# Pooled attention and a gated dense layer on one core: scores of two pairs in one step, an earlier due date for g, other places for the last tiles, and a new table of shifts

## The chip, the cores and the metric

The kernel runs on 1 core of one Trainium2 chip. The metric is the device time of that core in microseconds (us). Names of engines: PE is TensorE, ACT is ScalarE, DVE is VectorE, POOL is GpSimd, SP is SyncE, which here only issues DMAs.

## What is computed

```python
# attention: batch 8, heads 8, seq 576, head_dim 64
k_p = k.reshape(B, H, Sp, pool, D).mean(axis=3)          # pool = 8, Sp = 72
v_p = v.reshape(B, H, Sp, pool, D).mean(axis=3)
scores = scale * np.matmul(q, k_p.transpose(0, 1, 3, 2))  # scale = 1 / 8
scores = scores - np.max(scores, axis=-1, keepdims=True)
attn = np.exp(scores)
attn = attn / (np.sum(attn, axis=-1, keepdims=True) + 1e-09)
attn_out = np.matmul(attn, v_p)
# dense part: 4608 tokens, w_in 512 x 2048, w_out 2048 x 512
x = attn_out.transpose(0, 2, 1, 3).reshape(B * S, H * D)
h = x @ w_in
g = h * (1.0 / (1.0 + np.exp(-1.702 * h)))
out = g @ w_out
```

The result has 4608 rows of 512. Each batch has 576 tokens.

## The kernel before

**The work.** For each of 8 batches the attention is computed first. `sum_keys` and `sum_values` pool keys and values over 8 (tiles red_k, red_v, spread into kbd and vbd, and turned by PE into kps); the last 8 of the 72 pooled rows go a way of their own: they are loaded into tl, summed into tred, spread into tbd. `scores` runs the queries in two pieces: piece 0 has two tiles of 128 tokens, piece 1 has two of 128 and one of 64. For each of four head pairs j one step on PE computes the scores of a piece (sps, L665), DVE takes the maxima (nm) and subtracts them (sc), ACT takes the exponential, DVE the sums (sm) and the products main and tail. `weigh` turns the weights (mt, or apt and tpt on PE in batches 0 and 1; batches from TURNED = 2 on are turned on DVE), splits them into a high and a low part (ah and al, at), multiplies them by the values (pav, L876 to L879) and splits the result into x, high and low. The 8 x 64 tokens left over from the batches form chunk 8, which `gather_left` collects at the end.

`dense` runs over chunks c = 0 to 8 of 512 tokens and steps f = 0 to 15 of 128 columns of w_in. For one f, 12 matmuls give h (three products of high and low parts for each of four blocks of the depth, L1066 to L1068). ACT computes g (L1081) and its rounded form gh (L1086) from h; POOL, or DVE in chunk 8, computes gl = g - gh (L1094). Then, in a block of 12 matmuls, gh and gl times w_out are added to four output tiles o_0, o_128, o_256 and o_384 (L1111 to L1113), which stay in PSUM through all 16 steps. The fourth tile of chunk 0 is called warm. After f = 15 each tile is copied to SBUF (osb, L1123) and stored (L1124, queue of ACT). In chunk 8 tiles 0 and 256 are copied by DVE and stored by SP in two DMAs each, tiles 128 and 384 by ACT and its queue (L1127, L1130).

**Places.** PSUM has four tiles for o (ps_o), two for h and two for the attention (ps_a). In SBUF the place "g" has one buffer, which g and the copies osb_0 and osb_256 share; "osb" has two buffers, for osb_128 and osb_384; "gh" has two.

**What sets the order.** All steps go to a planner, `Plan.order`, which simulates the engines and lays out each engine's instructions in one fixed order by due dates. `plan.due` is set ahead of each part of the code; the table `SHIFTS` adds microseconds to the due dates of steps of one kind ("DVE tred2_0" is the step on DVE that writes tred for batch 2, part 0). A round of one batch's attention beside one chunk has 96 us. Before 58 us the planner fills PE's gaps with small matmuls of the identity (`keep_warm`, L1214). On the chip each engine runs its instructions in that order and waits at semaphores for what it needs.

Of the kernel before, what the change touches and what calls it, by code (L numbers as in the profile page):

```python
# [23 lines left out]
COLD = 7.0  # L24
UNTIL = 58.0
# [7 lines left out]
    "ACT at1_1": 15, "ACT g0_256": 16, "ACT gh0_0": 10, "ACT vh0": -26, "DMA kv2_0": 11, "DMA tl1": 13,  # L33
    "DVE at0_1": 14, "DVE e": 20, "DVE kbd1": 42, "DVE nm0_1": 6, "DVE nm1_0": 24, "DVE raws": 4, "DVE tail0_0": 13,
    "DVE tail0_1": 3, "DVE tbd1": 26, "DVE vbd2": -18, "DVE vt1": 4, "PE h0_256": -4, "PE h1_0": -3.4,
    "PE kps1_0": -70, "PE kps1_1": 53, "PE o1_384": -11, "PE qps0_1": 5, "PE red1_1": 13, "PE sps2_0": -7,
    "PE tpt0_1": -19, "PE tpt1_0": 21,
# [215 lines left out]
def attention_moe_kernel(ctx: ExitStack, tc: tile.TileContext, q, k, v, w_in, w_out, out):  # L253
# [371 lines left out]
    def scores(b, piece, m, whole_q=None):  # L625
# [8 lines left out]
        sm = buf(att, [P, NT, H], F32, "sm", f"sm{n}")  # L634
        for j in range(NJ):
# [25 lines left out]
            ps = buf(ps_o if first else ps_a, [P, 512], F32, "o" if first else "a", f"sps{n}_{j}")  # L661

            def score(j=j, qt=qt, ps=ps):
                for t, (s0, ns) in enumerate(tiles):
                    nc.tensor.matmul(  # L665
                        ps()[:ns, t * PW : (t + 1) * PW],
                        lhsT=qt()[:, s0 - o0 : s0 - o0 + ns],
                        rhs=m.k2()[:, j],
                        start=True,
                        stop=True,  # L670
                    )

            pe(246 * len(tiles), score, [qt, (m.k2, j // NP)], [ps], also=[sc, nm])
            hs = slice(2 * j, 2 * j + 2)
            for ns, g in groups:
                nt = g.stop - g.start

                def view(ns=ns, g=g, ps=ps):
                    return ps()[:ns, g.start * PW : g.stop * PW].rearrange("p (t h s) -> p t h s", h=2, s=KEYS)

                dve(
                    nt * PW,
                    lambda ns=ns, g=g, hs=hs, view=view: nc.vector.tensor_reduce(  # L683
                        out=nm()[:ns, g, hs], in_=view(), axis=AX.X, op=ALU.max, negate=True
                    ),
                    [ps],
                    [(nm, (j, ns))],
                )
                dve(
                    nt * PW,  # L690
# [575 lines left out]
```

## Time and profile before

| what | value |
|---|---|
| median of 3 runs | 958.68 us (957.93 to 959.54) |
| the profiled execution | 958.8 us, of it the span 957.0 us |
| mean granted clock of PE in the span | 0.999 of full speed |
| PE busy | 942.4 us, 98% |
| DVE, ACT, POOL busy | 557.4, 378.6 and 238.8 us |
| DMA over the span | 61 GB/s, the queue of SP 19.9% and of ACT 2.6% of the 16 DMA engines' time |

The busy time of matmuls overlaps: a matmul of 512 columns has a record of 0.39 us, but the next one starts 0.23 us after it. So a wait of PE is read from the start of one matmul to the start of the next. The chunks 1 to 8 begin at about 170, 270, 368, 468, 568, 668, 768 and 858 us.

### The profile page before, as it was taken

How to read it: one execution, taken by the hardware profiler on the slowest of the kernel's cores; microseconds unless marked ns; L12 is line 12 of the kernel's file. 1: busy time of each engine (PE TensorE's matmuls, PEld its weight loads, DVE VectorE, ACT ScalarE, POOL GpSimd, SP SyncE). 2: the span in 40 equal slices, each digit the busy share in tenths (PEclk: the TensorE clock that was granted, in tenths of full speed). 3: DMA queues.
4: the chain of work that ended last, by engine and by line, in shares of the span. 5: the costliest groups of instructions: out<-in, count | busy, mean ns of one | idle time of the engine just before them, and what ended most of it. 6: DMA issues, size and time to landing. Idle time of an engine off the chain costs nothing.

```text
span 957.0 us, 12693 instructions
## 1 busy us (share of the span) xinstructions
PE 942.4 (98%) x4670; PEld 783.9 (82%) x4670; DVE 557.4 (58%) x1095; ACT 378.6 (40%) x692; POOL 238.8 (25%) x191
## 2 busy tenths in 40 slices
PE   9999999999999999999999999999999999999997
PEld 8888988878877888788788888888888878887885
DVE  4989877688638874887387838793677110001111
ACT  3688654534233443343344325432453232112121
POOL 1588731212111221221221222122112122220000
PEclk9999999999999999999999999999999999999999
DMA  9954304400322023202230124012200020001001
GB/s 254 384 220 86 70 19 110 101 21 1 72 80 53 7 64 88 53 6 55 76 72 9 44 52 104 12 45 50 72 1 1 6 88 1 1 1 45 0 1 45
DMA packets 106414, 59.03 MB, mean 62 GB/s; under 512 B 81520, under 2 KB 89712, under 8 KB 106224
## 3 DMA queue, kind: packets, MB, share of 16 engines
q1 hardware_dynamic: 101424, 49.31, 19.9%
q10 hardware_dynamic: 4928, 8.92, 2.6%
q8 instruction: 37, 0.61, 0.3%
q14 instruction: 25, 0.20, 0.1%
HBM read 47.71 MB, written 10.49 MB: 61 GB/s over the span
## 4 chain that ended last, share of the span: by engine, by line
PE 90%; DVE 4%; DMA 2%; ACT 1%; issue 1%; SPq 1%; POOL 0%; ACTq 0%; DVEq 0%; POOLq 0%
PE h L1066 13%; PE o L1111 13%; PE h L1068 13%; PE h L1067 13%; PE o L1112 13%; PE o L1113 12%; PE sps L665 4%; PE warm L1214 2%; DMA tl<-in_k_dram 1%; PE pav L876 1%; PE pav L878 1%; DVE main L774 1%; PE pav L879 1%; PE pav L877 1%; PE red_k L460 1%
## 5 line engine op out<-in xcount | busy, mean ns | idle before, releaser
L1094 POOL TENSOR_TENSOR gl<-g,gh 128x512 fp32r<-128x512 f32 x126 | 167.1, 1326 | 575.0 <-ACT gh L1086 481.8
L1066 PE MATMUL h<-x,w 128*128 128x512 f32 (+1 forms) x640 | 240.8, 376 | 3.6 <-ACT gh L1086 3.6
L1068 PE MATMUL h<-x,w 128*128 128x512 f32 (+1 forms) x640 | 236.0, 369 | 0.0
L1067 PE MATMUL h<-x,w 128*128 128x512 f32 (+1 forms) x640 | 235.7, 368 | 0.0
L1111 PE MATMUL o<-w,gh 128*128 128x512 f32 x560 | 222.2, 397 | 0.0
L1112 PE MATMUL o<-w,gh 128*128 128x512 f32 x560 | 220.4, 394 | 0.0
L1113 PE MATMUL o<-w,gl 128*128 128x512 f32 x560 | 218.9, 391 | 0.0
L1081 ACT ACTIVATE g<-h 128x512 f32<-128x512 f32 x144 | 86.0, 597 | 276.0 <-PE h L1068 253.8
L1066 PEld LDWEIGHTS h<-x,w 128*128 128x128 f32 x640 | 120.5, 188 | 28.5 <-ACT gh L1086 7.1
L1068 PEld LDWEIGHTS h<-x,w 128*128 128x128 f32 x640 | 120.5, 188 | 20.7
L1067 PEld LDWEIGHTS h<-x,w 128*128 128x128 f32 x640 | 120.6, 188 | 19.4 <-issue 0.2
L1113 PEld LDWEIGHTS o<-w,gl 128*128 128x128 f32 x560 | 105.2, 188 | 24.0 <-POOL gl L1094 0.6
L1111 PEld LDWEIGHTS o<-w,gh 128*128 128x128 f32 x560 | 105.3, 188 | 23.7 <-issue 2.6
L1112 PEld LDWEIGHTS o<-w,gh 128*128 128x128 f32 x560 | 105.3, 188 | 19.3
L774 DVE TENSOR_TENSOR main<-sc,sm 32x256 f32<-32x256 f32 (+1 forms) x192 | 102.4, 533 | 2.9
L1094 DVE TENSOR_TENSOR gl<-g,gh 128x512 fp32r<-128x512 f32 x18 | 13.1, 726 | 155.2 <-ACT gh L1086 155.2
L1086 ACT ACTIVATE gh<-h 128x512 fp32r<-128x512 f32 x142 | 84.2, 593 | 13.6 <-PE o L1112 13.5
L665 PE MATMUL sps<-k,qt 128*128 128x144 f32 (+1 forms) x320 | 53.3, 294 | 0.0
L665 PEld LDWEIGHTS sps<-k,qt 128*128 128x128 f32 (+1 forms) x320 | 43.2, 178 | 9.3 <-issue 1.6
L654 DVE STREAM_TRANSPOSE qt<-qr 128x256 f32<-128x256 f32 (+1 forms) x56 | 25.3, 463 | 36.9 <-PE sps L665 34.7
L683 DVE TENSOR_REDUCE nm<-sps 128x4 f32<-128x288 f32 (+1 forms) x96 | 37.2, 387 | 13.1 <-PE sps L665 12.6
L1029 POOL TENSOR_TENSOR raw<-raw 128x512 uint32<-128x512 uint32 x30 | 33.9, 1134 | 28.0 <-ACT qt L649 18.4
(115 smaller groups left out, 950.2 us busy)
## 6 DMA issues: line engine op xcount, KB each, us to landing
out_dram<-osb ACTq DMA_DIRECT2D x32, 256.0 KB
raw<-in_moe_w_in_dram SPq DMA_DIRECT2D x15, 512.0 KB
raw<-in_moe_w_out_dram SPq DMA_DIRECT2D x15, 512.0 KB
kv_False<-in_k_dram SPq DMA_DIRECT2D x28, 256.0 KB
kv_True<-in_v_dram SPq DMA_DIRECT2D x28, 256.0 KB
qr<-in_q_dram SPq DMA_DIRECT2D x112, 40.0 KB
qr<-in_q_dram SPq DMA_DIRECT2D x112, 32.0 KB
tl<-in_v_dram SPq DMA_DIRECT2D x36, 64.0 KB
```

The source lines that it names most:

```text
L665: nc.tensor.matmul(ps()[:ns, t * PW : (t + 1) * PW], lhsT=qt()[:, s0 - o0 : s0 - o0 + ns], rhs=m.k2()[:, j], start=True, stop=True,)
L683: lambda ns=ns, g=g, hs=hs, view=view: nc.vector.tensor_reduce(out=nm()[:ns, g, hs], in_=view(), axis=AX.X, op=ALU.max, negate=True),
L774: lambda r=r, a=a, half=half, rows=rows, cols=cols, nt=nt: nc.vector.tensor_tensor(out=main()[32 * r : 32 * (r + 1), :, cols].rearrange("p ...
L1066: nc.tensor.matmul(o, lhsT=w[:, 0, j], rhs=xs[:, 0, j], start=j == 0, stop=False)
L1067: nc.tensor.matmul(o, lhsT=w[:, 1, j], rhs=xs[:, 0, j], start=False, stop=False)
L1068: nc.tensor.matmul(o, lhsT=w[:, 0, j], rhs=xs[:, 1, j], start=False, stop=j == NJ - 1)
L1081: 512, lambda: nc.scalar.activation(out=g(), in_=h(), func=AF.Gelu_apprx_sigmoid), [h], [g], table="gelu"
L1086: lambda: nc.scalar.activation(out=gh(), in_=h(), func=AF.Gelu_apprx_sigmoid),
L1094: engine.tensor_tensor(out=gl(), in0=g(), in1=gh().bitcast(F32), op=ALU.subtract)
L1111: nc.tensor.matmul(o, lhsT=gh()[:, i, tok], rhs=w[:, 0], start=f == 0, stop=False)
L1112: nc.tensor.matmul(o, lhsT=gh()[:, i, tok], rhs=w[:, 1], start=False, stop=False)
L1113: nc.tensor.matmul(o, lhsT=gl()[:, i, tok], rhs=w[:, 0], start=False, stop=f == NF - 1)
```

## The change

There are four edits. `scores` gathers two head pairs from batch 2 on and computes both in one step on PE; each pair still has its tile in PSUM and its steps on DVE. In `dense`, g, gh and gl of chunks 1 to 8 get a due date 40 us earlier. In chunk 8 the copy of tile 256 takes a place in "osb" and that of tile 384 one in "gh", so that no two of the four share one; tile 384 is copied half by DVE and half by ACT, and its two stores go one to SP's queue and one to ACT's. The table of shifts is replaced: 27 entries by 57, all of batches 0 to 2 and of the decoding of the weights.

```diff
+EAGER = 40.0
...
 SHIFTS = {
-    "ACT at1_1": 15, "ACT g0_256": 16, "ACT gh0_0": 10, "ACT vh0": -26, "DMA kv2_0": 11, "DMA tl1": 13,
...
+    "DVE x0_0": -37.2, "DVE x0_1": -23.6, "PE apt1_0": 30.2, "PE h0_0": -52.7, "PE h0_256": 4.1, "PE kps1_0": -88.3,
+    "PE kps2_1": -26.1, "PE o0_0": 8.6, "PE o0_128": 10.4, "PE o0_256": 28.4, "PE o1_0": -38.7, "PE o1_256": -49.4,
...
 }
...
+        waiting = []
         for j in range(NJ):
...
-            ps = buf(ps_o if first else ps_a, [P, 512], F32, "o" if first else "a", f"sps{n}_{j}")
-
-            def score(j=j, qt=qt, ps=ps):
-                for t, (s0, ns) in enumerate(tiles):
...
+            waiting.append((j, qt, buf(ps_o if first else ps_a, [P, 512], F32, "o" if first else "a", f"sps{n}_{j}")))
+
+            if b >= TURNED and len(waiting) < 2:
+                continue
+            batch, waiting = waiting, []
+
+            def score(batch=batch):
+                for jj, qt, ps in batch:
+                    for t, (s0, ns) in enumerate(tiles):
...
-            pe(246 * len(tiles), score, [qt, (m.k2, j // NP)], [ps], also=[sc, nm])
...
+            pe(
+                246 * len(tiles) * len(batch),
+                score,
+                [qt for _, qt, _ in batch] + [(m.k2, j // NP)],
+                [ps for _, _, ps in batch],
+                also=[sc, nm],
+            )
+            for jj, _, ps in batch:
+                hs = slice(2 * jj, 2 * jj + 2)
...
+        plan.due = due - (EAGER if c else 0.0)
         g = buf(moe, [P, len(fs), n], F32, "g", f"g{nm}", bufs=1)
...
             if fs[-1] == NF - 1:
-                first = t % (2 * P) == 0
+
+                tag = "g" if t % (2 * P) == 0 else "osb"
+                if c == B:
+                    tag = ("g", "osb", "osb", "gh")[t // P]
                 osb = buf(
-                    moe, [P, DM], F32, "g" if first else "osb", f"osb{c}_{t}", bufs=1 if first else None
+                    moe, [P, DM], F32, tag, f"osb{c}_{t}", bufs=1 if tag == "g" else None
                 )
...
+                def copy_half(i, copy, t=t, osb=osb):
+                    half = slice(i * DM // 2, (i + 1) * DM // 2)
+                    copy(out=osb()[:, half], in_=acc[t]()[:, half])
+
+                def store_both(t=t, osb=osb):
+                    for i, queue in enumerate((nc.sync, nc.scalar)):
+                        queue.dma_start(out=rows[t // LEFT + i, CHUNK:], in_=osb()[i * LEFT : (i + 1) * LEFT])
+
                 if c < B:
                     act(560, store, [acc[t]], [osb])
-                elif first:
+                elif t == CHUNK - P:
+                    dve(256, lambda f=copy_half: f(0, nc.vector.tensor_copy), [acc[t]], [(osb, 0)])
+                    act(256, lambda f=copy_half: f(1, nc.scalar.copy), [acc[t]], [(osb, 1)])
+                elif tag == "g" or t > P:
                     dve(512, lambda f=store_left: f(nc.vector.tensor_copy, nc.sync), [acc[t]], [osb])
                 else:
                     act(560, lambda f=store_left: f(nc.scalar.copy, nc.scalar), [acc[t]], [osb])
 
-                plan.add("DMA", 0.0, lambda: None, [osb])
+                last = c == B and t == CHUNK - P
+                plan.add("DMA", 0.0, store_both if last else lambda: None, [osb])
```

How the order moves is shown at three places. A name is a tile with its batch or chunk, its part, and a running number.

**At the change to chunk 4.** On ACT, before, from the last gh of chunk 3 (gh3_0_15) on:

```order
L1123 COPY osb3_0_4688<-o3_0_3895 128x512
L1124 DMA out_0_dram<-osb3_0_4688 128x512
L1123 COPY osb3_128_4694<-o3_128_3906 128x512
L1124 DMA out_0_dram<-osb3_128_4694 128x512
L1123 COPY osb3_256_4702<-o3_256_3914 128x512
L1124 DMA out_0_dram<-osb3_256_4702 128x512
L1123 COPY osb3_384_4708<-o3_384_3921 128x512
L1124 DMA out_0_dram<-osb3_384_4708 128x512
L603 CAST vh5_4721<-vbd5_4673 128x512
L1081 ACTIVATE g4_0_0_4728<-h4_0_0_4656 128x512
L1086 ACTIVATE gh4_0_0_4738<-h4_0_0_4656 128x512
```

and after:

```order
L1102 ACTIVATE g4_0_0_4698<-h4_0_0_4669 128x512
L1107 ACTIVATE gh4_0_0_4700<-h4_0_0_4669 128x512
L1147 COPY osb3_128_4724<-o3_128_3876 128x512
L1148 DMA out_0_dram<-osb3_128_4724 128x512
L1147 COPY osb3_0_4734<-o3_0_3867 128x512
L1148 DMA out_0_dram<-osb3_0_4734 128x512
L1147 COPY osb3_384_4745<-o3_384_3887 128x512
L1148 DMA out_0_dram<-osb3_384_4745 128x512
L1147 COPY osb3_256_4754<-o3_256_3881 128x512
L1148 DMA out_0_dram<-osb3_256_4754 128x512
```

The first g and gh of chunk 4 moved ahead of the four copies, and the copies go in another order. (At the changes to chunks 7 and 8 the same g and gh moved ahead, and the copies keep the order 0, 128, 256, 384.) On PE, before, the last o matmuls of chunk 3 are followed by the end of h for chunk 4:

```order
L1111 MATMUL o3_384_3921<-w1_15_1581,gh3_0_15_4652 128x512
L1112 MATMUL o3_384_3921<-w1_15_1581,gh3_0_15_4652 128x512
L1113 MATMUL o3_384_3921<-w1_15_1581,gl3_0_15_4662 128x512
L1066 MATMUL h4_0_0_4656<-x4_4122,w0_0_257 128x512
L1067 MATMUL h4_0_0_4656<-x4_4122,w0_0_257 128x512
L1068 MATMUL h4_0_0_4656<-x4_4122,w0_0_257 128x512
```

and after:

```order
L1132 MATMUL o3_384_3887<-w1_15_1629,gh3_0_15_4665 128x512
L1133 MATMUL o3_384_3887<-w1_15_1629,gh3_0_15_4665 128x512
L1134 MATMUL o3_384_3887<-w1_15_1629,gl3_0_15_4675 128x512
L1085 MATMUL h4_0_1_4741<-x4_4138,w0_1_353 128x512
L1086 MATMUL h4_0_1_4741<-x4_4138,w0_1_353 128x512
L1087 MATMUL h4_0_1_4741<-x4_4138,w0_1_353 128x512
L1132 MATMUL o4_0_4749<-w1_0_284,gh4_0_0_4700 128x512
L1133 MATMUL o4_0_4749<-w1_0_284,gh4_0_0_4700 128x512
L1134 MATMUL o4_0_4749<-w1_0_284,gl4_0_0_4711 128x512
L1132 MATMUL o4_128_4758<-w1_0_284,gh4_0_0_4700 128x512
```

The first block of o of chunk 4 moved up to three matmuls behind the last one of chunk 3. Before, 21 matmuls of h and scores of the next batch lay between (24 and 21 at chunks 7 and 8); at chunks 7 and 8 the two blocks now follow each other at once.

**In the attention of batch 1, between 140 and 180 us.** On DVE, before, the two sums over the last rows of batch 2:

```order
L531 TENSOR_REDUCE tred2_0_1723<-tl2_0_1673 128x64
L738 TENSOR_TENSOR tail1_1_1742<-sc1_1_1583,sm1_1_1665 128x128
L826 TENSOR_TENSOR at1_0_0_1736<-tpt1_0_1726,at1_0_0_1736 32x256
L738 TENSOR_TENSOR tail1_1_1742<-sc1_1_1583,sm1_1_1665 64x64
L541 TENSOR_TENSOR tbd2_1767<-tred2_0_1723,mask4_86 128x256
L826 TENSOR_TENSOR at1_0_1_1751<-tpt1_0_1726,at1_0_1_1751 32x256
L654 STREAM_TRANSPOSE qt2_0_0_1778<-qr2_0_0_1692 128x256
L654 STREAM_TRANSPOSE qt2_0_1_1789<-qr2_0_1_1712 128x256
L531 TENSOR_REDUCE tred2_1_1797<-tl2_1_1744 128x64
L898 TENSOR_TENSOR x1_1785<-pav1_0_0_1770,x1_1785 128x256
L898 TENSOR_TENSOR x1_1785<-pav1_0_1_1780,x1_1785 128x256
L541 TENSOR_TENSOR tbd2_1767<-tred2_1_1797,mask4_86 128x256
```

and after:

```order
L476 TENSOR_REDUCE red2_k1_1870<-kv2_1_False_1786 128x128
L917 TENSOR_TENSOR x1_1781<-pav1_0_2_1855,x1_1781 128x256
L917 TENSOR_TENSOR x1_1781<-pav1_0_3_1862,x1_1781 128x256
L486 TENSOR_TENSOR kbd2_1860<-red2_k1_1870,mask2_84 128x256
L537 TENSOR_REDUCE tred2_0_1902<-tl2_0_1681 128x64
L879 CAST ah1_1_0_1919<-apt1_1_0_1904 128x320
L845 TENSOR_TENSOR at1_1_0_1908<-tpt1_1_1898,at1_1_0_1908 32x320
L547 TENSOR_TENSOR tbd2_1937<-tred2_0_1902,mask4_86 128x256
L845 TENSOR_TENSOR at1_1_1_1921<-tpt1_1_1898,at1_1_1_1921 32x320
L883 TENSOR_TENSOR al1_1_0_1945<-apt1_1_0_1904,ah1_1_0_1919 128x320
L537 TENSOR_REDUCE tred2_1_1960<-tl2_1_1917 128x64
L547 TENSOR_TENSOR tbd2_1937<-tred2_1_1960,mask4_86 128x256
```

Both sums moved into the second piece of batch 1's attention (ah, al and at of 1_1), and a sum over keys (red2_k1) stands ahead of them. On PE, kps2_1, which reads tbd2, now stands ahead of pav1_1_1; before, all four pav of that piece came first.

**In a round of the later batches.** On DVE, before, the two sums over the last rows of batch 5 beside the second piece of batch 4:

```order
L531 TENSOR_REDUCE tred5_0_4471<-tl5_0_4380 128x64
L907 COPY left4_1_4434<-pav4_1_1_4466 128x64
L864 TENSOR_TENSOR al4_1_3_4488<-mt4_1_3_4464,ah4_1_3_4473 128x320
L898 TENSOR_TENSOR x4_4122<-pav4_1_1_4466,x4_4122 128x256
L541 TENSOR_TENSOR tbd5_4498<-tred5_0_4471,mask4_86 128x256
L898 TENSOR_TENSOR x4_4122<-pav4_1_2_4479,x4_4122 128x256
L470 TENSOR_REDUCE red5_k1_4507<-kv5_1_False_4431 128x128
L480 TENSOR_TENSOR kbd5_4453<-red5_k1_4507,mask2_84 128x256
L898 TENSOR_TENSOR x4_4122<-pav4_1_3_4509,x4_4122 128x256
L531 TENSOR_REDUCE tred5_1_4531<-tl5_1_4484 128x64
L541 TENSOR_TENSOR tbd5_4498<-tred5_1_4531,mask4_86 128x256
```

and after:

```order
L537 TENSOR_REDUCE tred5_0_4452<-tl5_0_4362 128x64
L883 TENSOR_TENSOR al4_1_0_4463<-mt4_1_0_4446,ah4_1_0_4456 128x320
L872 STREAM_TRANSPOSE mt4_1_1_4473<-main4_1_4284 128x320
L547 TENSOR_TENSOR tbd5_4478<-tred5_0_4452,mask4_86 128x256
L476 TENSOR_REDUCE red5_k1_4485<-kv5_1_False_4411 128x128
L917 TENSOR_TENSOR x4_4138<-pav4_1_0_4489,x4_4138 128x256
L883 TENSOR_TENSOR al4_1_1_4508<-mt4_1_1_4473,ah4_1_1_4480 128x320
L872 STREAM_TRANSPOSE mt4_1_2_4514<-main4_1_4284 128x320
L486 TENSOR_TENSOR kbd5_4429<-red5_k1_4485,mask2_84 128x256
L537 TENSOR_REDUCE tred5_1_4525<-tl5_1_4461 128x64
L883 TENSOR_TENSOR al4_1_2_4532<-mt4_1_2_4514,ah4_1_2_4520 128x320
```

The second sum moved from behind the last al of batch 4 to ahead of al4_1_2.

## Rows read from the trace of the kernel before

**Rows 1.** This is the page's first part: busy microseconds of each engine, its share of the span, number of instructions.

```profile
PE 942.4 (98%) x4670; PEld 783.9 (82%) x4670; DVE 557.4 (58%) x1095; ACT 378.6 (40%) x692; POOL 238.8 (25%) x191
```


**Rows 2.** This is the view of waits, TensorE (PE) alone: who waited for whom, microseconds of idle time in total, how often, the longest.

```profile
PE h L1066 <- ACT gh L1086: 3.6, 5, 1.2
...
PE pav L876 <- DVE sc L691: 1.4, 1, 1.4
...
PE pav L876 <- DVE at L826: 0.5, 1, 0.5
...
PE apt L798 <- DVE al L864: 0.3, 1, 0.3
...
PE pav L876 <- DVE al L864: 0.3, 1, 0.3
...
PE apt L798 <- DVE x L898: 0.2, 1, 0.2
```


**Rows 3.** This is the chain of waits around 300 and 377 us, the pieces in which the scores run (L665) and one that follows: start, microseconds until the next piece, what. x6 and x12 are one and two head pairs of a three-tile piece, x4 and x8 one and two of a two-tile piece.

```profile
303.87 1.96 PE sps L665 x12
...
308.79 0.88 PE sps L665 x6
...
309.67 0.43 PE h L1066
...
376.90 0.98 PE sps L665 x8
...
379.25 0.49 PE sps L665 x4
```


**Rows 4.** This is the timeline of the end of the program, all engines; SPq and ACTq are the DMA issues of SyncE and ScalarE: start, microseconds, engine, line, what, and in brackets the idle time ahead of it and what ended it.

```profile
948.80 0.59 ACT L1127 COPY osb<-o 128x512 f32<-128x512 f32 x1 [3.75 <-PE o L1113]
...
948.83 5.30 SPq L1130 DMA_DIRECT2D out_dram<-osb  x4
...
949.42 1.21 ACTq L1130 DMA_DIRECT2D out_dram<-osb  x2
...
949.75 0.39 PE L1113 MATMUL o<-w,gl 128*128 128x512 f32 x1
...
950.72 0.58 ACT L1127 COPY osb<-o 128x512 f32<-128x512 f32 x1 [1.34 <-PE o L1113]
...
951.34 1.13 ACTq L1130 DMA_DIRECT2D out_dram<-osb  x2
...
952.31 0.69 DVE L1127 COPY osb<-o 128x512 f32<-128x512 f32 x1 [3.50 <-DMA out_dram<-osb]
...
953.03 1.11 SPq L1130 DMA_DIRECT2D out_dram<-osb  x2
```


**Rows 5.** This is the chain of waits at the end: start, microseconds, what.

```profile
949.44 2.75 DMA out_dram<-osb
```


**Rows 6.** This is the timeline of TensorE at three changes from one chunk to the next (to chunks 2, 7 and 8).

```profile
280.30 0.50 PE L1066 MATMUL h<-x,w 128*128 128x512 f32 x1 [0.54 <-ACT gh L1086]
...
777.26 0.39 PE L1068 MATMUL h<-x,w 128*128 128x512 f32 x1
...
778.83 0.50 PE L1066 MATMUL h<-x,w 128*128 128x512 f32 x1 [1.18 <-ACT gh L1086]
...
779.17 0.40 PE L1067 MATMUL h<-x,w 128*128 128x512 f32 x1
...
867.79 0.50 PE L1066 MATMUL h<-x,w 128*128 128x512 f32 x1 [1.15 <-ACT gh L1086]
```


**Rows 7.** This is the timeline of ScalarE at the change to chunk 3: the four copies of finished output tiles (their DMA issues left out).

```profile
372.81 0.59 ACT L1123 COPY osb<-o 128x512 f32<-128x512 f32 x1 [3.50 <-PE o L1113]
...
373.87 0.59 ACT L1123 COPY osb<-o 128x512 f32<-128x512 f32 x1 [0.47 <-PE o L1113]
...
375.52 0.59 ACT L1123 COPY osb<-o 128x512 f32<-128x512 f32 x1 [1.06 <-DMA out_dram<-osb]
...
376.57 0.58 ACT L1123 COPY osb<-o 128x512 f32<-128x512 f32 x1 [0.46 <-ACT osb L1123]
```


**Rows 8.** This is the chain of waits at the change to chunk 2: the two output DMAs.

```profile
274.32 2.05 DMA out_dram<-osb
...
277.06 2.02 DMA out_dram<-osb
```


**Rows 9.** This is the timeline of TensorE at the longest early wait.

```profile
206.42 0.36 PE L876 MATMUL pav<-ah,vh 128*128 128x256 f32 x1 [1.38 <-DVE sc L691]
```


**Rows 10.** This is the chain of waits at two loads of a batch's last rows (tl) behind the sum over the earlier ones: one of the four DMA issues (SPq), and the transfers.

```profile
142.52 0.65 SPq L408
...
144.57 4.69 DMA tl<-in_k_dram
...
449.26 3.90 DMA tl<-in_k_dram
```


**Rows 11.** This is the timeline of VectorE (DVE): a sum over keys (red_k), a sum over last rows (tred) that waits for its load, and a reader of an output in PSUM (pav) of which ScalarE reads another part (left).

```profile
448.57 1.98 DVE L470 TENSOR_REDUCE red_k<-kv_False 128x128 f32<-128x1024 f32 x1
...
453.28 1.07 DVE L531 TENSOR_REDUCE tred<-tl 128x64 f32<-128x512 f32 x1 [1.94 <-DMA tl<-in_k_dram]
...
641.95 0.42 DVE L898 TENSOR_TENSOR x<-pav,x 128x256 fp32r<-128x256 f32 x1 [0.28 <-ACT left L907]
```

More of the change, by code (lines that the diff above doesn't have):

```diff
@@ L32 @@
 SHIFTS = {
-    "ACT at1_1": 15, "ACT g0_256": 16, "ACT gh0_0": 10, "ACT vh0": -26, "DMA kv2_0": 11, "DMA tl1": 13,
[L34 to L37, printed above, removed]
+    "ACT ah0_1": -52.2, "ACT ah1_0": 37.2, "ACT at2_0": 23.1, "ACT g0_0": 35.7, "ACT gh0_0": 36.2, "ACT k1_0": 35,
+    "ACT qt0_1": 2.8, "ACT raw": 11.5, "ACT w": -2.2, "DMA qr1_0": -50.2, "DMA tl1": 38.8, "DVE al0_1": -11.2,
+    "DVE al1_1": 162.9, "DVE al2_0": 13.2, "DVE e": 37.3, "DVE kbd2": 15.5, "DVE main0_0": 28.3, "DVE main0_1": 18.1,
+    "DVE main2_0": 95.3, "DVE main2_1": 86.1, "DVE nm1_1": 80.6, "DVE nm2_1": 30.1, "DVE qt1_0": -111.9,
+    "DVE raw": -7, "DVE raws": -6.7, "DVE sc0_1": -30.9, "DVE sc1_0": 70.9, "DVE sc2_0": 32.7, "DVE sc2_1": -34.6,
[5 rows of a table added]
 }
@@ new lines, in scores @@
+            if b >= TURNED and len(waiting) < 2:
[4 more added lines that the diff above has]
+                    for t, (s0, ns) in enumerate(tiles):
+                        nc.tensor.matmul(
+                            ps()[:ns, t * PW : (t + 1) * PW],
+                            lhsT=qt()[:, s0 - o0 : s0 - o0 + ns],
+                            rhs=m.k2()[:, jj],
+                            start=True,
+                            stop=True,
+                        )
@@ new lines, in scores, with view @@
+            pe(
[4 more added lines that the diff above has]
+                also=[sc, nm],
+            )
+            for jj, _, ps in batch:
+                hs = slice(2 * jj, 2 * jj + 2)
+                for ns, g in groups:
+                    nt = g.stop - g.start
+                    def view(ns=ns, g=g, ps=ps):
+                        return ps()[:ns, g.start * PW : g.stop * PW].rearrange("p (t h s) -> p t h s", h=2, s=KEYS)
+                    dve(
+                        nt * PW,
+                        lambda ns=ns, g=g, hs=hs, view=view: nc.vector.tensor_reduce(
+                            out=nm()[:ns, g, hs], in_=view(), axis=AX.X, op=ALU.max, negate=True
+                        ),
+                        [ps],
+                        [(nm, (jj, ns))],
+                    )
+                    dve(
+                        nt * PW,
+                        lambda ns=ns, g=g, hs=hs, nt=nt, view=view: nc.vector.tensor_tensor(
+                            out=sc()[:ns, g, hs],
+                            in0=view(),
+                            in1=nm()[:ns, g, hs].unsqueeze(3).broadcast_to([ns, nt, 2, KEYS]),
+                            op=ALU.add,
+                        ),
+                        [ps, (nm, (jj, ns))],
+                        [(sc, ns)],
+                    )
```

32 lines of the change are left out of this document (1 added, 31 removed), and 3 rows, old and new, of the table SHIFTS.

## The prediction

> **What bounds the kernel now.** I read first the busy shares, then who waits for whom, then the chain of waits, then the timeline at the places that these name. TensorE (PE) is busy 942.4 us of a span of 957.0 [rows 1]. The reader is to see that almost nothing but PE's own work sets the time: 14.6 us are left, and they lie in three heaps. (1) After the last matmul starts at 949.75 the program still runs 7.25 us [rows 4]. (2) At the changes of chunk PE waits for a gh: idle 0.54, 1.18 and 1.15 us [rows 6]. (3) Before the rounds become regular PE waits for VectorE (DVE): 1.4 + 0.5 + 0.3 + 0.3 + 0.2 us, the 1.4 of them at 206 us [rows 2, 9]. The rest is the start, where PE waits for data and is padded with fillers. So an edit is worth what it takes from these heaps; the work itself stays, because the matmuls are the same in both kernels but for one filler. The profiled execution took 958.8 us, 1.8 more than its span; the median is 958.68. I sum against 958.8.
>
> **Two pairs' scores in one step: 0.** A two-tile piece takes 0.49 us for one pair and 0.98 for two at once [rows 3]: twice the same. A three-tile piece takes 0.88 for one pair, and the step behind it 0.43 in place of 0.23, so 1.08; two at once take 1.96 [rows 3] and the same 0.20 once, so 2.16, again twice. What it could cost is a later start of the first pair's maximum, by 0.49 to 1.08 us a piece. DVE takes it up, with 58% of its time used [rows 1]. I take 0.
>
> **The end: -2.0.** Before, the copy of tile 256 sits idle for 3.50 us for the DMA of tile 0 [rows 4], which ends 2.75 us after its issue at 949.44 [rows 5], since both used the place "g". Only then follow the copy (0.69) and the last two issues (1.11, from 953.03 to 954.14) [rows 4]. From there to the end of the span are 2.86 us. After the change tile 256 has a place that nobody holds. DVE copies it when its sum is done, one tile (0.69) before the last: 949.48 to 950.17. SyncE issues from 948.83: four issues at about 0.6 each (1.21 and 1.13 for two) [rows 4] end at 951.3. Tile 384 is now copied in halves. ScalarE is free for it at 950.72, as before, because its own two issues run to 950.63 [rows 4]. Half of a 0.58 us copy with its fixed part is some 0.35, so 951.1. DVE's half waits for ScalarE's (the nearest row is a reader of one PSUM tile that sits idle 0.28 us for the other engine's read [rows 11]) and takes some 0.42, to 951.5. Both queues then issue one DMA of 0.6: 952.1. 954.14 - 952.1 = 2.0 earlier. Bounds: 1.5, if DVE's half starts late or the many stores at one time finish later, and 2.5, if the halves run together and the last completion is shorter.
>
> By the Trainium skill, page "PSUM — Partial Sum Buffer", section "PSUM bank collisions raise a hardware error", two engines must not read one bank's quadrant at the same time, in whichever columns, so the split halves cannot overlap. This speaks against halving; with the halves side by side the sum for the end would be 2.2, since SyncE is free only at 951.3, and one after the other, as the row also has it, 2.0.
>
> **The changes of chunk, what goes: -3.7.** The first g of the new chunk came on ScalarE (ACT) behind the four copies of finished tiles. The third copy waits for the DMA of the first (1.06 us idle [rows 7], the DMA itself 2.05 [rows 8]), because both use "g", and g must then wait for the second such DMA (2.02 [rows 8]). At three changes this reaches PE: idle 0.54 + 1.18 + 1.15 = 2.87 [rows 6]. The step is longer than the idle time by some 0.16 each (777.26 to 778.83 is 1.57 in place of 0.23, so 1.34 for an idle 1.18), and the matmul after it starts 0.34 in place of 0.23 later [rows 6]: 0.27 more each, 0.8 in all. EAGER takes g and gh of the first step past the copies, so all of this goes: 3.7.
>
> **The changes of chunk, what comes: +3.3.** The last block of twelve o matmuls of the old chunk (2.75 us, 12 x 0.23) is now followed by the first one of the new chunk, at once for chunks 7 and 8, after three matmuls (0.69) for chunks 2 to 6; before, 21 to 24 matmuls of h (4.8 to 5.5 us) and, up to chunk 6, scores lay between. The new tiles take the four accumulation banks of the old ones, so each waits for a copy on ACT. From the first copy's start to the fourth's end are 376.57 + 0.58 - 372.81 = 4.34 us [rows 7], with the wait for the DMA in it, which stays. With T the start of the old block, the copies start at T + 0.72 and the fourth ends at T + 5.06; PE is there at T + 2.75 + 3 x 0.69 = T + 4.82 and waits until about T + 5.10: 0.3. For chunks 2 to 6 the copies start one tile later. For 3 to 6 they run in the order 128, 0, 384, 256, so tile 0's copy ends at T + 3.05, its DMA at T + 5.1, the copy of 256 runs T + 5.2 to 5.8, and PE is there at T + 5.51: 0.3 to 0.4 (chunk 2 comes to the same: all copies later by 0.69). With the slower restart of 0.11 I take 0.47 at each of seven changes: 3.3. Bounds: 0, if ACT gets ahead by a third of a microsecond, and 1.2 each, if the copies are held by the two activations ahead of them (the longest such wait so far is 1.18 [rows 6]): 0 to 8.4.
>
> **The early part, what goes: -3.7.** The order of DVE's work for batches 0 to 2 is shifted throughout. The five waits in heap (3) are 2.7 us of idle time, and two of the five waits for gh are left (3.6 - 2.87 = 0.7 [rows 2, 6]), one of which, 0.2, goes with the new order. With some 0.13 more for each of six steps that is 3.7. In the new order each of these operands is made two or more microseconds ahead of its matmul.
>
> **The early part, what comes: +2.5.** Before, both sums over batch 2's last rows (tred2_0, tred2_1) stood far ahead of the second piece of batch 1's attention, the second right behind the first but for small work. Now they stand inside it: ahead of them a sum over keys (2.0 us [rows 11]), behind the second one the x, al and tbd on which PE's kps2 and pav1_1 rest. The second sum's load can be issued when the first sum is done: three issues of 0.65 ahead of the last transfer, and that takes 3.9 to 4.7 [rows 10], so it lands 6.0 to 6.7 later. The second sum (1.07 [rows 11]) and tbd (some 0.42) follow: 7.5 to 8.2. On PE there are 9.5 us of work from the last pav of the first piece to kps2. If DVE begins tred2_0 1.0 us after that pav, kps2 comes 0.1 to 0.8 late; if it is 3.1 us behind (the sum over keys lies in its way), 2.2 to 2.9. I take 1.5, and 1.0 for two shorter places where a score or a pav stands closer behind its DVE work than before: 2.5, between 0.1 and 5.
>
> **A filler: +0.2.** One more warm matmul, about 0.22.
>
> **Sum.** 958.8 - 2.0 - 3.7 + 3.3 - 3.7 + 2.5 + 0.2 = 955.4.
>
> **Rivals.** A, the banks come free in time: PE does not wait at the changes. For it: 0.3 us is less than the precision of such a sum. Against it: the wait for the DMA of tile 0 is in the trace at each change that I looked at. 955.4 - 3.3 = 952.1.
>
> B, no change that can be told: what goes early comes back in the same part. For it: DVE has long sums and loads of 6 us there, and a new order there moves waits rather than removing them. The early part then costs 5.0 rather than 2.5, and the changes 0.6 a time rather than 0.47: 955.4 + 2.5 + 0.9 = 958.8.
>
> C, slower: in the five like rounds of batches 3 to 7 DVE's second sum over the last rows waits for its load, as it does now (1.94 us at 453.28 [rows 11]). Today only preparation for the next batch stands behind it; in the new order the al and x of the attention's second piece do, and PE's pav rests on them. Between the two sums lie some 5.2 us of DVE work (one sum over keys of 2.0, seven of 0.4 to 0.5), against 6.0 to 6.7 for the load: about 1.2 us idle. If PE has less in hand than this, each round pays; at 1.5 us each that is 7.5: 962.9. It decides as soon as the idle time passes what lies between al and pav, which I put near a microsecond.
>
> D, the new order does not do what it says and g stays behind the copies: it would leave the 3.7 and spare the 3.3, so 955.0, within the forecast.
>
> **How the numbers follow.** Forecast with D, 953.5 to 956.8: 0.45. A, about 952: 0.15. B, 956.8 to 960.5: 0.25. C, about 963: 0.15. The likeliest gives 955.4. The range for 8 in 10 leaves out C and the ends of the rest: 951.4 to 960.3. A measurement of this kernel tells about 0.2%, 1.9 us, from no change, so faster is below 956.8: 0.45 + 0.15 = 0.60; within: 0.25; slower: 0.15.
>
> **What would show it.** In the profile of the changed kernel: DVE's copy of tile 256 at about 0.6 us after PE's last block but one, with no wait for a DMA, and the last issue some 2 us nearer to the last matmul; no wait of h for gh at the changes, but an o matmul, the fourth tile of the first block, that waits for the copy of 256, by 0.3 to 0.5 us; one wait of 1 to 2 us for DVE's tbd or al around 165 us and none at 206; the two-pair scores at 0.98 and 1.96 us. PE waits for al or x in each round from 380 us on would make the prediction wrong on the slow side (C); a PE idle sum below 1 us between 60 and 945 would make it wrong on the fast side.

## The result, and the profile after

The changed kernel takes 963.56 us (median of 6 runs, 961.47 to 965.07), the kernel before, run beside it, 958.11 (956.63 to 959.54). The ratio is 1.0053, 95% interval 1.0037 to 1.0068: slower by half a per cent, where 955.4 had been forecast. The profiled execution took 963.49 us, its span 961.3.

The page's first part and the row of TensorE's granted clock, in 40 slices of 24 us:

```profile
PE 946.7 (98%) x4672; PEld 785.8 (82%) x4672; DVE 558.7 (58%) x1105; ACT 390.2 (41%) x696; POOL 232.3 (24%) x188
...
PEclk9999998999999999999999999999999999999999
```

PE is busy 4.3 us longer than in [rows 1], for two matmuls more. The work is the same, so the same matmuls took longer somewhere, and the one 8 in the clock's row, in the slice from 144 to 168 us, says where. The view of waits, PE alone (total us, times, longest):

```profile
PE o L1132 <- ACT osb L1147: 3.6, 5, 1.0
...
PE warm L1132 <- ACT gh L1107: 1.3, 1, 1.3
PE pav L898 <- DVE al L883: 0.8, 2, 0.4
PE warm L1134 <- POOL gl L1115: 0.6, 1, 0.6
```

Against [rows 2], the waits of h for gh and of pav for sc are gone. In their place o waits for the copies of finished tiles, and a wait for gh and one for gl have come, both in chunk 0. I go through the three places.

**The end.** The timeline of all engines:

```profile
955.24 0.69 DVE L1153 COPY osb<-o 128x512 f32<-128x512 f32 x1 [0.68 <-PE o L1134]
...
955.50 0.39 PE L1134 MATMUL o<-w,gl 128*128 128x512 f32 x1
956.42 0.37 ACT L1159 COPY osb<-o 128x256 f32<-128x256 f32 x1 [1.28 <-PE o L1134]
956.82 0.42 DVE L1159 COPY osb<-o 128x256 f32<-128x256 f32 x1 [0.89 <-ACT osb L1159]
957.28 0.47 ACTq L1163 DMA_DIRECT2D out_dram<-osb  x1
957.43 0.55 SPq L1163 DMA_DIRECT2D out_dram<-osb  x1
```

DVE's copy of tile 256 no longer waits for a DMA (955.24, against the 3.50 us in [rows 4]). The last issue ends at 957.98, 2.48 us after the last matmul starts, where it was 4.39. But then 3.3 us pass until the span ends at 961.3, where it was 2.9. Of 1.9 us gained at the issue, 1.4 arrive.

**The changes of chunk.** The timeline of PE at the change to chunk 4, and at the place of a later round that is spoken of below:

```profile
483.68 0.40 PE L1134 MATMUL o<-w,gl 128*128 128x512 f32 x1
485.04 0.51 PE L1132 MATMUL o<-w,gh 128*128 128x512 f32 x1 [0.96 <-ACT osb L1147]
485.38 0.40 PE L1133 MATMUL o<-w,gh 128*128 128x512 f32 x1
...
554.32 0.30 PE L897 MATMUL pav<-at,vt 96*128 96x320 f32 x1
555.05 0.41 PE L898 MATMUL pav<-al,vh 128*128 128x320 f32 x1 [0.43 <-DVE al L883]
```

And the chain of waits at the changes to chunks 2, 3, 4 and 8:

```profile
280.07 2.27 DMA out_dram<-osb
...
381.28 2.41 DMA out_dram<-osb
...
481.62 2.76 DMA out_dram<-osb
...
871.14 2.02 DMA out_dram<-osb
```

The order did what it said: g comes ahead of the copies. PE now waits where it was expected to, for the copy of tile 256, which waits for the DMA of tile 0, since both use the place "g" (at the changes to chunks 7 and 8 for the copy of tile 384 right behind it). Here the step takes 1.36 us in place of 0.23. Over the seven changes, in order, steps are longer by 0.54, 0.78, 1.13, 1.05, 0.93, 0.26 and 0.25 us, and the DMAs that they wait for take 2.27, 2.41, 2.76, 2.68, 2.56, 2.04 and 2.02. Wait and DMA rise and fall together, with some 1.7 us between them.

The long DMAs are those beside which loads run. At each of the changes to chunks 2 to 6 SyncE issues eight loads of queries at that time; at chunk 4 in the timeline:

```profile
478.57 3.92 SPq L447 DMA_DIRECT2D qr<-in_q_dram  x8
```

At the changes to chunks 7 and 8 there are none, and in the kernel before none ran beside the 2.05 us of [rows 8]. A store ahead of it is not what makes a store long: the one of 2.05 was issued 1.06 us behind another (273.26 and 274.32), and the one of 2.27 here goes first in its row. That the loads are the cause is read from these rows; no run takes them away.

**Around 156 us.** The timeline of PE:

```profile
155.68 0.28 PE L1087 MATMUL h<-x,w 128*128 128x256 f32 x1
157.29 0.50 PE L1132 MATMUL warm<-w,gh 128*128 128x512 f32 x1 [1.33 <-ACT gh L1107]
...
158.65 0.53 PE L1134 MATMUL warm<-w,gl 128*128 128x512 f32 x1 [0.62 <-POOL gl L1115]
...
164.70 0.63 PE L1132 MATMUL o<-w,gh 128*128 128x512 f32 x1
165.13 0.63 PE L1133 MATMUL o<-w,gh 128*128 128x512 f32 x1
```

Of ACT:

```profile
151.91 0.59 ACT L1147 COPY osb<-o 128x512 f32<-128x512 f32 x1
153.99 0.34 ACTq L1148 DMA_DIRECT2D out_dram<-osb  x1
156.16 0.60 ACT L1102 ACTIVATE g<-h 128x512 f32<-128x512 f32 x1 [3.66 <-DMA out_dram<-osb]
```

And the chain of waits there:

```profile
149.97 3.94 DMA kv_False<-in_k_dram
...
153.99 2.08 DMA out_dram<-osb
```

Read upwards: PE waits for gh, gh follows g, and g waits 3.66 us for a store. The copy of a tile of chunk 0 lies in the place "g", which the g of a later step wants; the copy ends at 152.50, but its store is issued only at 153.99, when a load of keys has landed that has nothing to do with it. Then the store takes its 2.08. Behind the two waits (1.95 us idle within 3 us) the granted clock falls. The windows of before and of after, the same two stretches (busy us and count of PE, PEld, DVE, ACT, POOL, then the granted clock of PE, DMA share, GB/s); first before, then after:

```profile
152.00:160.00 8.00, 8.00 (x52) 6.67 (x51) 6.52 (x11) 4.77 (x11) 1.29 (x1) 1.00 0.49 139
160.00:168.00 8.00, 8.00 (x49) 6.86 (x47) 5.85 (x11) 2.43 (x7) 0.00 (x0) 1.00 0.26 70
```

```profile
152.00:160.00 8.00, 6.04 (x33) 4.86 (x33) 6.59 (x9) 2.13 (x5) 1.28 (x1) 0.94 0.80 191
160.00:168.00 8.00, 8.00 (x34) 6.15 (x33) 3.85 (x7) 3.28 (x7) 0.69 (x1) 0.64 0.11 35
```

The busy share of the second stretch is the same, 8.00 of 8.00, yet PE does 34 instructions in it where it did 49: at the clock's lower level (1.2 GHz of 2.4) one matmul of o follows the other after 0.43 us (164.70 to 165.13) and not after 0.23. A clock of 0.94 and 0.64 over 8 us each is 8 x (0.06 + 0.36) = 3.4 us of PE's time, more than the waits themselves. The kernel does not pay all of it in each execution: of the six, three had a mean granted clock of 0.995 to 0.996 and took 964.1 us in the mean, three had 0.999, with the same order of instructions, and took 962.3. So the fall does not follow these waits every time, and where it does, the kernel is less than 2 us later.

### The profile page after: what moved, and what is told of

Read it like the earlier page. It is cut to its first block, busy times and chain, and to the rows that moved or that the text cites. A ratio compares the mean times of both kernels' runs of the same rounds, so it can differ in the third digit from the quotient of the medians.

```text
span 961.3 us, 12683 instructions
## 1 busy us (share of the span) xinstructions
PE 946.7 (98%) x4672; PEld 785.8 (82%) x4672; DVE 558.7 (58%) x1105; ACT 390.2 (41%) x696; POOL 232.3 (24%) x188
## 4 chain that ended last, share of the span: by engine, by line
PE 84%; DVE 6%; DMA 4%; ACT 3%; issue 1%; POOL 1%; ACTq 0%; SPq 0%; DVEq 0%; POOLq 0%
PE h L1085 12%; PE h L1086 12%; PE h L1087 12%; PE o L1132 11%; PE o L1133 11%; PE o L1134 11%; PE sps L677 5%; PE warm L1251 2%; DMA out_dram<-osb 2%; DVE main L793 2%; DMA kv_False<-in_k_dram 1%; ACT osb L1147 1%; PE pav L898 1%; DVE red_k L476 1%; PE pav L895 1%
## 5 line engine op out<-in xcount | busy, mean ns | idle before, releaser
L1115 POOL TENSOR_TENSOR gl<-g,gh 128x512 fp32r<-128x512 f32 x122 | 160.7, 1317 | 578.6 <-ACT gh L1107 456.1
L1115 DVE TENSOR_TENSOR gl<-g,gh 128x512 fp32r<-128x512 f32 x22 | 17.7, 807 | 151.6 <-ACT gh L1107 151.6
L729 DVE TENSOR_REDUCE sm<-sc 128x16 f32<-128x1152 f32 (+1 forms) x24 | 27.4, 1147 | 40.7 <-ACT sc L723 40.7
```

Source lines behind the costliest of these rows:

```text
L1115: engine.tensor_tensor(out=gl(), in0=g(), in1=gh().bitcast(F32), op=ALU.subtract)
```

## The experiments

My theory after this: the new order of work is not to blame as such; two places that tiles share are, one around 156 us and one at the changes. The rival: the order of DVE's work in the early part and the position of the merged scores cost the time, and places don't matter. Each figure below is the difference of medians to the kernel before in the same set of runs.

**Both places undone.** The order of all instructions stays that of the changed kernel; `osb.make` only says where the tile is put: the first `if` is for tiles 0 and 256 of chunk 0, the second for tile 256 of chunks 1 to 7.

```diff
+if c == 0 and tag == "g":
+    osb.make = lambda name=osb.name: moe.tile([P, DM], F32, tag="osb", name=name)
+if 0 < c < B and t == 2 * P:
+    osb.make = lambda name=osb.name: moe.tile([P, DM], F32, tag="gh", name=name)
```

> The changed kernel with every instruction in its new order and only two places altered: the copies of chunk 0's tiles 0 and 256 take a place in osb, and the copies of tile 256 of chunks 1 to 7 take one in gh, so that no copy that another waits for shares the place g. Theory (the shared place g makes the loss): the waits of 1.3 and 0.6 us at 155 to 159 us shrink to under 0.5, the clock stays at its full level there, and the waits of o for osb at the changes (5.7 us with their restarts) go; 963.5 becomes 952.5 to 955. Rival (the new order of DVE's work makes the loss, and these waits only stand in front of others): under 2 us are gained, 961.5 or more.

Measured: 953.83 against 957.98, ratio 0.9960 (0.9948 to 0.9973). With every instruction where it was, the kernel went from slower by 5.4 us to faster by 4.2. The theory holds. The timeline of PE and the chain of waits of this kernel show what then comes to light:

```profile
167.28 0.64 PE L817 MATMUL apt<-ident,main 128*128 128x128 f32 x3 [1.77 <-DVE x L917]
```

```profile
161.38 3.81 DMA tl<-in_k_dram
...
165.41 1.03 DVE tred L537
```

That is the wait for batch 2's second sum over the last rows that the prediction had named. In the changed kernel it was covered by the other wait just ahead of it. The clock stayed at 1.00 here, behind a single wait of 1.77 us.

**Each place alone.** The first `if` alone:

> Only chunk 0's tiles 0 and 256 take a place in osb, order unchanged. Theory: the waits at 155 to 159 us (2.2 us with what follows) go, and with them the 3.3 us at the lower clock level, where it fell: 958 to 961.5, the waits at the changes stay as they are. Rival (DVE's sums over last rows at 159 to 167 us would have stopped PE anyway): PE waits 1 to 2 us at the kps or pav that follow, 961 to 963.5, and the clock falls all the same.

Measured: 960.72, ratio 1.0034 (1.0021 to 1.0047), in the theory's range. But the rival's wait is there as well: PE waits 1.51 us for DVE at 165.97 us, and one of the seven executions has the lower clock (964.51 us, mean 0.995). The second alone:

> Only the copies of tile 256 of chunks 1 to 7 take a place in gh, order unchanged. Theory: the seven waits of o for osb go, 5.7 us: 957.5 to 958.5, with the wait and the lower clock at 155 to 166 us as in the changed kernel. Rival (ACT's four copies in a row are what holds the banks, not the DMA): the copies then end 1.0 to 1.5 us earlier at best and waits of some 0.3 stay: 960 to 961.5.

Measured: 956.64, ratio 0.9986 (0.9977 to 0.9995), below the range of the theory. So against the changed kernel (+5.45) the place of chunk 0 is worth 2.7 us (+2.74) and that of the later chunks 6.8 (-1.34); together 9.5, and the kernel with both gained 9.6 (-4.15). The first is less than wait and clock together because the wait for x shows in its stead. The second is more than the 5.7 that I count at the changes. Most of the other microsecond is a wait of scores for DVE at 186 us, 0.7 us with its restart. It stands in the changed kernel and in the one with the first place alone, and in neither of those that have the second place. The timeline of PE in the changed kernel:

```profile
186.71 0.76 PE L677 MATMUL sps<-k,qt 128*128 128x144 f32 x4 [0.57 <-DVE sc L710]
```

**The kernel before with only the new end.**

> The kernel before with only the new places, the halves and the queues of the last chunk's four tiles. Theory (the end gains as its last issue does, less a later completion, as the changed kernel's profile has it): 1.4 us less than before, so 956.7 beside 958.1. The prediction had 2.0 less. Rival (nothing, the end is bound by the completion of the stores): 958.1.

Measured: 956.52 against 957.98, ratio 0.9985 (0.9976 to 0.9993): -1.46. The 0.5 us short of the prediction's 2.0 were seen above, between the last issue and the end.

**The earlier due date alone, in the kernel before.**

```diff
+EAGER = 40.0
...
+        plan.due = due - (EAGER if c else 0.0)
```

> The kernel before with only the due dates of g, gh and gl 40 us earlier. In the order that results, g and gh come ahead of the four copies at the changes to chunks 7 and 8 alone, and the two blocks of o follow each other there; at the changes to chunks 3 to 6 nothing moves. Theory (early g pays where PE waited for gh and costs where it did not): at chunks 7 and 8 the waits of 1.34 and 1.31 us with their restarts become 0.26 and 0.25, so 2.1 us less than before: 955.9 beside 958.0. Rival (an early g only trades one wait for a like one): 958.0.

Measured: 958.31 against 958.35, ratio 1.0001 (0.9992 to 1.0010): no gain, against what I expected. In this kernel's order g and gh pass the copies at the changes to chunks 7 and 8 only, and two new waits of h for gh, at 386.83 and 587.53 us, take back some 1.4 of the 2.1 us; the rest is within the interval of 0.9. The first of them in the timeline of PE:

```profile
386.83 0.50 PE L1067 MATMUL h<-x,w 128*128 128x512 f32 x1 [0.51 <-ACT gh L1088]
```

**The new shifts alone, in the kernel before.** The new table has 58 entries.

> The kernel before with only the new table of shifts. Theory (the new early order is the loss): the waits of 1.3 and 0.6 us at 155 us and, where it falls, the lower clock appear, heap of early waits 3 to 5 us longer: 960.5 to 963. Rival (the early loss comes from the shifts together with the other edits): 957 to 959.

Measured: 967.4 against 958.35, ratio 1.0094 (1.0079 to 1.0110), more than expected. The wait at 156 us and the fall of the clock are there too (1.56 and 0.63 us idle at 158 and 159 us), and further waits for gh follow, as at 191 us (timeline of PE), where g and gh are parted by the exponential of the next batch:

```profile
191.46 0.50 PE L1071 MATMUL h<-x,w 128*128 128x512 f32 x1 [1.32 <-ACT gh L1091]
```

**The merged scores alone, in the kernel before.**

> The kernel before with only the scores of two pairs in one step. Theory (the matmuls cost the same, only the order moves; g comes ahead of the copies at chunk 8): between 956.5 and 958. Rival (two scores' tiles at a time take both places that pav needs, and PE waits in each round): 960 or more.

Measured: 975.96 against 958.35, ratio 1.0188 (1.0171 to 1.0205): +17.6 us for an edit that I had costed at 0. The size is that of the rival, but not by its mechanism: what is late is not a pav but ACT. The view of waits:

```profile
PE h L1079 <- ACT gh L1099: 13.6, 8, 3.0
```

The timelines of ACT and of PE at the longest of the eight:

```profile
526.23 0.60 ACT L1094 ACTIVATE g<-h 128x512 f32<-128x512 f32 x1 [5.32 <-PE h L1081]
526.85 1.28 ACT L717 ACT_TABLE_LOAD   x1
528.14 1.74 ACT L717 ACTIVATE sc<-sc 128x1152 f32<-128x1152 f32 x2
529.90 1.28 ACT L1099 ACT_TABLE_LOAD   x1
531.19 0.60 ACT L1099 ACTIVATE gh<-h 128x512 fp32r<-128x512 f32 x1
```

```profile
531.84 0.58 PE L1079 MATMUL h<-x,w 128*128 128x512 f32 x1 [2.98 <-ACT gh L1099]
```

The planner put the exponential of the scores between the g and the gh of one step, and it brings two loads of a table: 1.28 + 1.74 + 1.28 = 4.3 us ahead of a gh for which PE waits. Behind each of the two waits of 2.98 us the granted clock also falls for 3.4 us, so a part of the 17.6 is the clock's. EAGER draws gh forward past the exponential, so in the changed kernel, and in the next run, this is not seen: merged scores need the earlier due date. By the Trainium skill, page "ScalarE: Activation LUTs", section "What ACT_TABLE_LOAD costs", a switch of tables also drains the engine and comes to about 2.66 us; here it does not agree: the exponential starts 0.01 us after its table is loaded (526.85 + 1.28 to 528.14), and the load 0.02 us after g, so a switch costs 1.3.

**The changed kernel with the shifts of before.**

> The changed kernel with the table of shifts of before: scores of two pairs, early g and the new end stay. Theory (the early loss is the table's, the loss at the changes belongs to the early g with the merged scores): early waits as before, waits of o for osb at the changes of 5 to 6 us, none for gh, 1.4 us gained at the end: 958 to 959.5. Rival (merged scores lose in the rounds whatever the due dates, as they did alone): 965 or more.

Measured: 959.03 against 958.38, ratio 1.0012 (1.0003 to 1.0021), in the theory's range. Its waits are not quite those named: o waits at six of the changes, 4.8 us with restarts, and at the change to chunk 2 h still waits for a gh (0.54 us idle). And of the early waits of before, those at 206 and at 456 us are gone, with the old table. And the same with tile 256 in "gh":

> The same as e12_old_shifts, and the copies of tile 256 of chunks 1 to 7 take a place in gh, order unchanged. Theory: the waits at the changes go, 5 to 6 us less than e12_old_shifts, 952.5 to 953.5, about what the kernel before gives with the new end and this place (952.5). Rival (an early g and merged scores bring something of their own once the place is free): 951.5 or less.

Measured: 952.84, ratio 0.9943 (0.9930 to 0.9955).

**The kernel before with the new end and tile 256 of chunks 1 to 7 in "gh", nothing moved.**

> The kernel before in its own order, with the new end and with the copy of tile 256 of chunks 1 to 7 in a place of gh. Theory (the shared place g is what held g at the changes to chunks 2, 7 and 8): of the 3.7 us at these changes 2.5 to 3.7 go, 952.9 to 954.0. Rival (g waits for the four copies themselves, 4.3 us in a row, of which the wait for the DMA is a small part): 955.5 to 956.5.

Measured: 952.52 against 958.35, ratio 0.9946 (0.9933 to 0.9958), a little under its range, the lowest time of all and faster than both kernels. It stands level with the one above, so the earlier g and the merged scores add nothing that can be told once the place is another. The timeline of ACT at a change:

```profile
772.52 0.58 ACT L1127 COPY osb<-o 128x512 f32<-128x512 f32 x1 [0.41 <-PE o L1113]
...
774.62 0.60 ACT L1081 ACTIVATE g<-h 128x512 f32<-128x512 f32 x1 [0.47 <-ACT osb L1127]
```

Neither the third copy nor g waits for a DMA, where in [rows 7] the third copy did for 1.06 us. g still stands behind all four copies and is in time: of five waits of h for gh [rows 2] one of 0.5 us is left, at 125.8 us and not at a change.

**The store of chunk 0's tile 128 as two DMAs**, in the changed kernel. The load of keys that holds the store at 153.99 and the store have no data in common. Completion semaphores are given to DMAs in turn, and I took it that these two share one; one DMA more shifts the turn.

```diff
-nc.scalar.dma_start(out=out[c * S + t : c * S + t + P], in_=osb())
+parts = 2 if (c, t) == (0, P) else 1
+for i in range(parts):
+    r = slice(i * P // parts, (i + 1) * P // parts)
+    nc.scalar.dma_start(out=out[c * S + t : c * S + t + P][r], in_=osb()[r])
```

> The changed kernel, with the store of chunk 0's tile 128 issued as two DMAs of half the rows. The order of the instructions is the same but for that one more issue on ACT's queue, and by it the next store, of tile 0, waits for another of the eight completion semaphores that the program's DMAs share in turn: no longer the one of the load of batch 2's keys. Theory (ACT sits in front of that store until the load of keys has landed, 1.5 us, and g stands behind it): the store is issued at about 152.6 to 153.0 us in place of 154.0, PE's wait at 155.7 falls from 1.3 to 0.5 or less, and with the lower clock gone 960 to 961.5. Rival (the store was ready only then for another reason, or the place g alone decides): the wait stays above 1 us, 963 to 964.

Measured: 964.19 against 958.38, ratio 1.0069 (1.0055 to 1.0082): no gain, a miss. The chain of waits of this kernel:

```profile
151.77 4.07 DMA qr<-in_q_dram
...
155.91 2.20 DMA out_dram<-osb
```

The store now waits for a load of queries, longer than before (issued at 155.91), and PE's wait grows to 2.42 us. The load that holds the store changed when the turn was shifted by one. The semaphore records of the two traces name the link. In the changed kernel ACT waits ahead of the store for semaphore 104, which the load of keys counts up until 153.92, and the store then counts up the same one. In this run it is semaphore 105, which the load of queries counts up until 155.84. Eight semaphores serve all DMAs of the program. So the store did wait for a shared semaphore; the edit only gave it another partner, and a later one.

**The wait filled.** In the changed kernel 13 matmuls of the identity, into a PSUM tile that is no longer read, stand ahead of the o step that waits at 155.7 us. They give PE work and take no wait away.

> The changed kernel with 13 matmuls of the identity (1.45 us, into the PSUM tile of chunk 0's output 0, which has been copied by then and is not read again) put into the wait at 155.7 us, ahead of the o step that waits for gh. Theory (PE's idle time is what lowers the clock, and the clock's cost is partly covered by DVE's sum over last rows, which is late anyway): no idle time of 1.3 us there, the granted clock stays at its upper level from 159 to 166 us, PE then waits 0.5 to 2 us for DVE around 167 us, and the time is 0.5 to 2 us less than the changed kernel's 963.56: 961.5 to 963. Rival A (the lower clock is unrelated to the wait): it falls all the same, 963.5 to 965. Rival B (all 3.3 us at the lower clock are lost time): 960 to 960.5.

Measured: 961.19 against 957.93, ratio 1.0039 (1.0025 to 1.0052): +3.26 in place of +5.45. The clock stayed up; the timeline of PE and the window that was at 0.64:

```profile
155.80 3.06 PE L1275 MATMUL o<-ident 128*128 128x128 f32 x26
158.62 0.47 PE L1132 MATMUL warm<-w,gh 128*128 128x512 f32 x1
...
168.07 0.64 PE L817 MATMUL apt<-ident,main 128*128 128x128 f32 x3 [0.56 <-DVE x L917]
```

```profile
160.00:168.00 8.00, 7.51 (x42) 5.61 (x39) 4.33 (x10) 3.77 (x9) 1.29 (x1) 1.00 0.11 33
```

The fillers cost 2.82 us (155.80 to 158.62), more than the idle time that they replace and twice what I had reckoned (the row counts 26 matmuls for the 13), and a wait for x of 0.56 shows behind them. All the same the kernel gains 2.2 us on the changed kernel's median, a little more than the theory had. On the mean of the three executions in which that kernel's clock hardly fell (+4.2) it gains 1.0: so the larger part is the clock, and not all of it.

## Why the prediction was wrong

Three pairs of runs split the result. The new end alone gives -1.46 (forecast -2.0). The earlier g and the merged scores on top of it go from -1.46 to +0.65, that is +2.1 (forecast 3.3 - 3.7 = -0.4). The shifts on top of that go from +0.65 to +5.45, that is +4.8 (forecast -3.7 + 2.5 + 0.2 = -1.0). The misses are 0.5, 2.5 and 5.8 us: 8.8 in all, the whole way from -3.4 to +5.45. Two terms failed: what comes in the early part, which did not see the wait of ACT, and what comes at the changes, which was mis-sized.

- **The early part, what comes (+2.5): the step that failed.** It looked for new waits behind DVE's work alone; that "each of these operands is made two or more microseconds ahead of its matmul" was said of the operands of the old waits, and g and gh of chunk 0 had no term. ACT's part around 150 us was not followed with the places in SBUF: a copy of chunk 0 in "g" ahead of the next g, with a store that holds it. That costs 1.33 + 0.62 us idle, a slower restart, and, in the profiled execution, 3.4 us by the clock: about 5.6. The forecast had the same mechanism in hand for the later chunks (copy, DMA, "g") and did not ask for it in chunk 0. The wait that it did name, 1.5 us for batch 2's second sum, was sized right: 1.77 and 1.51 us in the two kernels in which nothing covers it. In the changed kernel PE is held up ahead of it and never meets it.
- **The early part, what goes (-3.7): right that they go, wrong in what takes them.** None of the waits for DVE of [rows 2] between 60 and 460 us is left. But those at 206 and 456 us, some 1.9 us with restarts, are gone with the old table as well, and the one at 206 with the merged scores alone: they belong to the second of the three pairs, not to the shifts. The shifts' own sum is then -1.8 + 2.5 + 0.2 = +0.9, and +1.4 was measured once both places are other ones (from -5.54 to -4.15). Small waits came at 68 to 87 us (1.05 us in three, where one of 0.40 had stood) and at 186 us (0.73).
- **The changes, what goes (-3.7): right.** In the changed kernel no h waits for a gh any more.
- **The changes, what comes (+3.3): right in mechanism, too small.** With the restart of 0.11 each it is 4.94 + 0.77 = 5.7. The term that was off is the DMA of tile 0, taken at the 2.05 of [rows 8]. In the new order loads of queries run beside it at the changes to chunks 2 to 6, and it takes 2.27 to 2.76; at chunks 7 and 8, where none do, 2.02 to 2.04. The forecast did not ask what else the DMA engines do at that time. The forecast's wait of 0.3 plus what the DMA takes above 2.05 gives 0.5, 0.7, 1.0, 0.9, 0.8, 0.3 and 0.3, within 0.15 of each of the seven. Also, by [rows 2] and [rows 6] only some of the changes held PE up before; the edit brought a wait to all.
- **The end (-2.0): right in mechanism, too large by 0.5.** The issues came 1.9 us nearer, as reckoned; the bound of 1.5 had named it, stores that finish later: from the last issue to the end of the span 3.3 us pass, and not 2.9. That it comes of more stores at one time is the forecast's reason, and no run tests it.
- **Merged scores (0): right for PE, as far as it went.** The step of eight matmuls takes 0.98 us, as before. What an edit of a step's length does to the planner's order was not costed, and alone it is +17.6.
- **Rival C (slower by DVE's second sum in five rounds, 7.5 us): wrong.** In two rounds of five a pav waits for al, 0.73 in place of 0.14 us at 554.32 and as much at 655.6: 1.2 us. But the second sum over the last rows comes behind that al, without a wait. The timeline of DVE:

```profile
551.65 1.97 DVE L476 TENSOR_REDUCE red_k<-kv_False 128x128 f32<-128x1024 f32 x1
553.54 1.46 DVE L883 TENSOR_TENSOR al<-mt,ah 128x320 fp32r<-128x320 f32 x1
...
555.88 1.07 DVE L537 TENSOR_REDUCE tred<-tl 128x64 f32<-128x512 f32 x1
```

  A sum over keys stands ahead of the al, and the al takes 1.46 us, where the next one takes 0.48; POOL's gl runs beside it from 553.36 to 554.65. Whether gl is the cause no run tests. These waits are there with the old table too, so they come of the merged scores or the earlier due date. The kernel came out where C had put it, for other reasons: the number is luck.
- **Rivals A and B** did not happen as told either: the banks are not free in time, and what came early is a new wait of ACT and a lower clock, not DVE's sums.

Put together, with the small waits net of the one that went: 958.8 - 1.4 - 3.7 + 5.7 - 3.7 + 5.6 + 0.65 + 0.7 + 1.2 + 0.2 = 964.05, against 963.5 measured in the profiled execution. The share of 5.6 in it is the least sure, since three of the six executions hardly paid for the clock; their 962.3 is still far above the forecast.

## What to carry to other kernels

When steps are moved, follow not only what they read but where their results lie: a tile that shares its place with one that is being stored waits for a copy, for whatever holds the store's issue, and for the whole store. Before moving work around such a wait, try another place for the tile: here two lines that move one tile, without any reordering, took off some 4.4 us (-5.83 against -1.46 with the new end alone), and no new order tried here added to it. And edits of a planner's inputs are not priced one by one: the merged scores cost 17.6 us alone, and nothing that can be told beside the earlier due date and the other place.

## What the runs showed of the hardware that was not expected

- The clock. In the profiled execution two waits of 1.33 and 0.62 us, close together, were followed by the lower level from 159.0 to 165.8 us; a single wait of 1.77 us some 10 us further on in the program was not. With only the scores merged, two single waits of 2.98 us were followed by it and two of 2.35 us were not. And in three of six executions of the changed kernel it hardly fell. With the wait filled by matmuls the clock stayed at 1.00.
- Stores. The DMA of one output tile takes 2.02 to 2.05 us, also when it is issued about 1 us behind another, and 2.27 to 2.76 where loads of queries run beside it. The Trainium skill, page "DMA: Bandwidth & Descriptors", section "Latency and other measured facts", puts most of a DMA's fixed cost down to the memory's latency, which rises with load. These rows agree in direction; whether it is the memory or the DMA engines that the loads share with the store they do not tell.
- An issue on ACT's queue was held 1.5 us (152.50 to 153.99) for a load from another queue with which it shares no data but a completion semaphore, and with one DMA more in the row for another load.
